# A cast to a DRAM scratch placed 5 steps later in the program, and its transposes 7 steps later

## The chip, the cores and the metric

The kernel runs on 1 core of one Trainium2 chip. The metric is the device time of one execution in microseconds (us). The core's engines are TensorE (PE, with PEld for its weight loads), VectorE (DVE), ScalarE (ACT), GpSimd (POOL) and SyncE (SP). Each works off its own queue in order.

## The reference

Two stages follow each other: a causal convolution along the sequence with 7 taps, whose weights are a softmax over the taps and one set for each of 8 heads (24 channels each), and a feed-forward block with a SiLU gate.

```python
def _attn_ref(x, weight):                 # x: (8, 4096, 192), weight: (8, 7)
    B, S, D = x.shape
    H, K = weight.shape
    group = D // H
    w = softmax(weight)                   # over the 7 taps
    x_pad = np.concatenate([np.zeros((B, K - 1, D)), x], axis=1)
    idx = np.arange(S)[:, None] + np.arange(K)[None, :]
    x_unf = x_pad[:, idx, :].reshape(B, S, K, H, group)
    return np.einsum('hk,bskhg->bshg', w, x_unf).reshape(B, S, D)

def _moe_ref(x, w_gate, w_val, w_out):    # x: (32768, 192), d_ff = 1536
    g = x @ w_gate
    silu = g * (1.0 / (1.0 + np.exp(-g)))
    return silu * (x @ w_val) @ w_out
```

## The kernel before, in words

The 32768 tokens are cut into 16 units of 2048 tokens (numbered from 0), each unit into 4 blocks of 512, and each block's feed-forward into 12 steps, one for each 128 of the 1536 hidden features. So there are 768 steps, 48 for a unit. Unit v begins at step 48v; a step's place in its block is called its step 0 to 11.

**A step** (`gate_val`, L768 to L789): six matmuls of 64x128 weights by 512 tokens, two at a time on the two row halves, fill the PSUM banks gate and val; ACT makes sig = silu(gate) (L786); DVE makes the product h = sig * val (L788). At steps 1, 4, 7 and 10 of a block a slot follows (`slot`, `down`, L803): 24 small matmuls that project products made earlier down to 192 channels. The slot at step 1 takes the products of the block before, among them that of its step 11; the one at step 4 ends that block, and ACT and DVE copy it (L860, L861) for the output DMA on SP (L864, three buffers). The banks gate and val have three buffers, so the matmuls of a step wait for the h of three steps before.

**The convolution** is made ahead of its use, and for unit 2 and the units from 4 on (`POOLED`) beside the steps, on ACT, DVE and POOL:

- `cast_x` (L590): POOL issues one DMA that reads the unit's x (2048 tokens and 16 ahead of them), turns it to 16 bit and writes it to a DRAM scratch xs (two buffers). For every second unit SP first writes zeros there (L583).
- `turn_x` (L605): SP issues transposes of 128 channels by 528 tokens from the scratch to SBUF, eight for a unit, in eight buffers for each of the two kinds (channels 0 to 127 of a block; channels 64 to 191, of which the upper half of a pair of blocks is used). `join_x` (L609) copies the second block's channels of a pair beside the first's, two for a unit.
- `queue_jobs` enters six jobs for a unit, in the order block 0, pair 0, block 1, block 2, pair 1, block 3. Each job sums seven shifted products. ACT makes the first into total (L682) and one or two more as part; DVE adds two by one instruction each, which reads the shifted x and total and writes total (L657, called a DVE step here); POOL adds ACT's parts (L632) and then makes the last two or three products itself (L647, piece) and adds each (L632). The last add writes the result in 16 bit, pxc for a block or y for a pair.
- `place` (L706): SP copies the results into the 64-row pieces that the gate and val matmuls read, 16 steps ahead of the block's first step.

**What sets the order.** Everything is recorded in one pass over the steps, and `seq` ties each instruction behind the one before it on its engine, so the place in the program is the order of each queue. `pooled_work` takes an ACT step and a DVE step from the lists at the steps 1, 7 and 10 of a block (ACT at step 4 too). POOL's part of a job is recorded when the DVE and ACT steps that it needs have been. `planned` (L722) puts a unit's cast, transposes and jobs on the plan by step number; in L957 the plan's entries of a step are recorded at that step's end. Before the change, for units from 4 on, the cast stands at step 48v - 115, the eight transposes and two joins at every second step from 48v - 105 to 48v - 87, and the jobs are entered at 48v - 89. The first ACT step of a unit's first job is recorded at 48v - 80 (48v - 83 for unit 4).

Of the kernel before, what the change touches and what calls it, by code (L numbers as in the profile page):

```python
# [10 lines left out]
def kernel(  # L11
# [564 lines left out]
    def cast_x(u):  # L576
        rows = XP + UT
        xs[u] = dpool.tile([rows, D], fp16, tag="xs", name="xs")
        flat = xs[u].rearrange("t d -> (t d)")
        skip = XP if u % upb == 0 else 0  # L580
        if skip:
            seq(
                nc.sync.dma_start(  # L583
                    out=flat[0 : XP * D].rearrange("(a n) -> a n", n=P),
                    in_=fill[0 : XP * D // P, :],
                )
            )
        n = (rows - skip) * D // P
        seq(
            nc.gpsimd.dma_start(  # L590
                out=flat[skip * D : rows * D].rearrange("(a n) -> a n", n=n),
                in_=bass.AP(
                    tensor=x_flat.tensor,
                    offset=(u * UT - XP + skip) * D,
                    ap=[[n, P], [1, n]],
                ),
            )
        )

    def turn_x(u, i, at):  # L600
        rows = xs[u][TB * i : TB * i + TB + XP]
        tiles = (x01, x12)[at // Q]
        tag = f"x{at // Q}"
        t = cpool.tile([P, TB + XP], fp16, tag=tag, name=tag, bufs=8)
        seq(nc.sync.dma_start_transpose(out=t, in_=rows[:, at : at + P]))  # L605
        tiles[u, i] = t

    def join_x(u, i):
        seq(nc.sync.dma_start(out=x12[u, 2 * i + 1][0:Q], in_=x12[u, 2 * i][Q:P]))  # L609
# [104 lines left out]
    def queue_jobs(u):  # L714
        for job in (
            ("block", 0), ("pair", 0), ("block", 1),
            ("block", 2), ("pair", 1), ("block", 3),
        ):
            conv_job(u, *job)
        placing.extend((u, i) for i in range(UB))  # L720

    def planned(v):  # L722
        s0 = ustep * v
        turns = (
            (0, 0), (0, Q), (1, Q), None, (1, 0), (2, 0), (2, Q), (3, Q), None, (3, 0)
        )
        if v == 2:
            cast, jobs = 21, 55
            times = (36, 36, 36, 38, 39, 39, 41, 41, 43, 43)
        elif v == 3:  # L730
            cast, jobs = 60, 56
            times = range(66, 86, 2)
        else:
            cast, jobs = s0 - 115, s0 - 89
            times = range(s0 - 105, s0 - 85, 2)
        plan.setdefault(cast, []).append(lambda: cast_x(v))
        for m, turn in enumerate(turns):
            if turn:
                todo = lambda turn=turn: turn_x(v, *turn)
            else:  # L740
                todo = lambda i=m // 8: join_x(v, i)
            plan.setdefault(times[m], []).append(todo)
        plan.setdefault(jobs, []).append(lambda: queue_jobs(v))
# [149 lines left out]
    for v in POOLED:  # L893
        planned(v)
# [106 lines left out]
```

## Time and profile before

| | us |
|---|---|
| median of 3 runs (lowest to highest) | 776.02 (775.38 to 777.03) |
| the profiled execution's own time | 777.99 |
| its span, first to last instruction | 776.2 |
| busy in the span: PE, DVE, ACT, POOL | 769.2, 706.2, 623.6, 597.6 |
| idle of POOL ahead of an add that waits for DVE (27 times) | 40.0 |
| wait of SP's queue at transposes, for casts (11 times) | 113.7 |
| a cast, from issue to landing, with zeros ahead or without (medians) | 6.7, 7.4 |

The granted TensorE clock was 0.999 of full speed. A row of the timeline gives the start in us from the span's start, the duration in us (of all where several equal ones are merged, "x2"), engine and line, output and input with their shapes, and in brackets the idle time ahead of it with what ended it. DVE rows overlap their neighbours by some 0.08 us, since the next instruction starts while the last one drains.

### The profile page before, as it was taken

The page shows a single profiled execution, that of the slowest core. Times are in us where ns is not written, and L with a number is a line of the kernel's source. Part 1 is how long each engine was busy: PE and PEld are TensorE (multiplying, and loading weights), DVE is VectorE, ACT ScalarE, POOL GpSimd, SP SyncE. Part 2 cuts the span into 40 slices and gives each one's busy share as a digit, 9 for nine tenths or more (in the row PEclk, how much of TensorE's full clock was granted, in tenths as well). Part 3 has the DMA queues.
Part 4 walks back from the last instruction along what each step waited for, and adds up shares of the span by engine and source line. Part 5 has one row for each costly group of instructions (what it writes and reads, how often), then busy time and mean ns, then how long its engine had stood idle before and what let it go on. Part 6 is the DMA issues. An engine that isn't in the chain of part 4 may idle for free.

```text
span 776.2 us, 27834 instructions
## 1 busy us (share of the span) xinstructions
PE 769.2 (99%) x11179; PEld 595.7 (77%) x11179; DVE 706.2 (91%) x1034; ACT 623.6 (80%) x1067; POOL 597.6 (77%) x551
## 2 busy tenths in 40 slices
PE   8999999999999999999999999999999999999997
PEld 5666666668878888788787888878888787887886
DVE  6677898999999999999999999999999999997775
ACT  6576888888888888888888888888888888876664
POOL 9100697799999999999999999999999999993000
PEclk9999999999999999999999999999999999999999
DMA  9959755745544535355343453635445344221211
GB/s 139 185 115 128 179 117 104 152 102 115 108 101 91 113 91 112 81 118 118 84 109 93 91 119 77 112 91 109 101 100 115 79 109 93 64 69 35 70 57 42
DMA packets 143652, 79.31 MB, mean 102 GB/s; under 512 B 89147, under 2 KB 143043, under 8 KB 143043
## 3 DMA queue, kind: packets, MB, share of 16 engines
q1 hardware_dynamic: 130690, 61.58, 35.3%
q0 software_dynamic: 12832, 15.96, 13.1%
q8 instruction: 87, 1.43, 0.8%
q14 instruction: 43, 0.34, 0.1%
HBM read 31.92 MB, written 37.83 MB: 90 GB/s over the span
## 4 chain that ended last, share of the span: by engine, by line
PE 98%; DVE 0%; issue 0%; ACT 0%; DVEq 0%
PE val L777 41%; PE acc L803 32%; PE gate L777 23%; PE warm L877 1%; PE turn L445 0%; DVE h L788 0%; PE cv L476 0%; PE cv L387 0%; PE acc L824 0%; ACT tme L405 0%; ACT wide L345 0%; ACT o_sb L969 0%; PE taps L332 0%; PE ctap L565 0%; PE tapbank L301 0%
## 5 line engine op out<-in xcount | busy, mean ns | idle before, releaser
L786 ACT ACTIVATE sig<-gate 128x512 f16<-128x512 f32 x768 | 458.6, 597 | 134.6 <-PE gate L777 82.0
L788 DVE TENSOR_TENSOR h<-sig,val 128x512 f16<-128x512 f16 x768 | 496.1, 682 | 60.3 <-PE gate L777 34.1
L777 PEld LDWEIGHTS <-w 64*128 64x128 f16 x4608 | 337.3, 110 | 137.0 <-issue 3.1
L777 PE MATMUL gate<-pxc,w 64*128 64x512 f16 x1872 | 438.8, 376 | 0.0
L777 PE MATMUL val<-pxc,w 64*128 64x512 f16 x1872 | 437.6, 376 | 0.1
L803 PE MATMUL acc<-wo,h 64*128 64x192 f16 x6096 | 330.4, 243 | 0.0
L803 PEld LDWEIGHTS <-h 64*128 64x128 f16 x6096 | 301.1, 94 | 30.3 <-issue 1.4
L632 POOL TENSOR_TENSOR total<-total,part 128x512 f32<-128x512 f32 x130 | 172.9, 1330 | 46.7 <-DVE total L657 40.0
L657 DVE SCALAR_TENSOR_TENSOR total<-x,both_taps,total 128x512 f32<-128x512 f16 x156 | 187.6, 1203 | 0.0
L632 POOL TENSOR_TENSOR total<-total,piece 128x512 f32<-128x512 f32 x104 | 147.6, 1419 | 8.7
L647 POOL TENSOR_SCALAR piece<-x,both_taps 128x512 f32<-128x512 f16 x182 | 150.8, 828 | 0.0
L777 PE MATMUL val<-xc,w 64*128 64x512 f16 x432 | 102.1, 376 | 0.5 <-issue 0.5
L777 PE MATMUL gate<-xc,w 64*128 64x512 f16 x432 | 102.1, 376 | 0.0
L682 ACT ACTIVATE part<-x,both_taps 128x512 f32<-128x512 f16 x130 | 92.8, 714 | 0.0
L632 POOL TENSOR_TENSOR pxc<-total,piece 128x512 f16<-128x512 f32 x52 | 67.8, 1303 | 4.3
L682 ACT ACTIVATE total<-x,both_taps 128x512 f32<-128x512 f16 x78 | 55.7, 714 | 0.0
L632 POOL TENSOR_TENSOR y<-total,piece 128x512 f16<-128x512 f32 x26 | 33.1, 1273 | 2.2
L861 DVE COPY o_sb<-acc 128x384 f32<-128x384 f32 x63 | 34.5, 547 | 0.0
L860 ACT COPY o_sb<-acc 128x384 f32<-128x384 f32 x63 | 29.7, 472 | 5.3 <-PE acc L803 5.3
L98 POOL DMA_DIRECT2D x<-in_x_dram x6 | 5.1, 873 | 24.5 <-ACT sig L786 24.5
L504 POOL COPY tm<-tm 128x1280 f16<-128x1280 f16 x2 | 2.5, 1251 | 19.2 <-DVE tm L493 19.2
L590 POOL DMA_DIRECT2D xs<-in_x_dram x13 | 7.2, 557 | 0.0
(67 smaller groups left out, 75.4 us busy)
## 6 DMA issues: line engine op xcount, KB each, us to landing
out_dram<-o_sb SPq DMA_DIRECT2D x63, 384.0 KB
pxc<-pxc SPq DMA_DIRECT2D x104, 64.0 KB
pxc<-y SPq DMA_DIRECT2D x104, 64.0 KB
xs<-in_x_dram POOLq DMA_DIRECT2D x7, 768.0 KB, 6.7
xs<-in_x_dram POOLq DMA_DIRECT2D x6, 774.0 KB, 7.4
x<-in_x_dram POOLq DMA_DIRECT2D x6, 480.0 KB, 9.1
scr<-tm SPq DMA_DIRECT2D x14, 130.0 KB
x<-x SPq DMA_DIRECT2D x26, 66.0 KB
```

Source lines behind the costliest of these rows:

```text
L590: nc.gpsimd.dma_start(out=flat[skip * D : rows * D].rearrange("(a n) -> a n", n=n), in_=bass.AP(tensor=x_flat.tensor, offset=(u * UT - XP ...
L632: nc.gpsimd.tensor_tensor(job["dst"] if k == K - 1 else total, total, part, op=ALU.add)
L647: nc.gpsimd.tensor_scalar(part, shifted(k), scalar1=job["tap"][:, k : k + 1], scalar2=1.0, op0=ALU.mult, op1=ALU.mult,)
L657: nc.vector.scalar_tensor_tensor(job["total"], shifted(k), job["tap"][:, k : k + 1], job["total"], op0=ALU.mult, op1=ALU.add,)
L682: nc.scalar.activation(part, shifted(k), AF.Copy, scale=job["tap"][:, k : k + 1])
L777: nc.tensor.matmul(o, w16[m][p0 : p0 + Q, k, e::E], xc[b][k][p0 : p0 + Q, 0:TB], start=(k == 0), stop=(k == SL - 1),)
L786: silu[n] = seq(nc.scalar.activation(sg, g, AF.Silu)).ins
L788: seq(nc.vector.tensor_tensor(hj, sg, v, op=ALU.mult))
L803: nc.tensor.matmul(acc[b][bank][:, s, :], hj[p0 : p0 + Q, ts(2 * bank + s, P)], wo16[p0 : p0 + Q, j, :], start=(not second and j == 0 and ...
L860: seq(nc.scalar.copy(o_sb[:, 0:2, :], acc[b][0]))
L861: seq(nc.vector.tensor_copy(o_sb[:, 2:4, :], acc[b][1]))
L877: nc.tensor.matmul(warm[:, 0:width], fill, fill.unsqueeze(1).to_broadcast([P, width // P, P]), start=True, stop=True, skip_group_check=True,)
```

## The change

For the units from 4 on the cast is recorded 5 steps later, at 48v - 110, and the transposes and joins 7 steps later, from 48v - 98 to 48v - 80. The step at which the jobs are entered stays.

```diff
@@ -731,8 +731,8 @@
             cast, jobs = 60, 56
             times = range(66, 86, 2)
         else:
-            cast, jobs = s0 - 115, s0 - 89
-            times = range(s0 - 105, s0 - 85, 2)
+            cast, jobs = s0 - 110, s0 - 89
+            times = range(s0 - 98, s0 - 78, 2)
         plan.setdefault(cast, []).append(lambda: cast_x(v))
         for m, turn in enumerate(turns):
             if turn:
```

On POOL each cast then stands behind the adds and products of one job more: for units from 5 on behind those of a pair job instead of ahead of them, and ahead of the next block job's. On SP the transposes and joins stand behind some outputs and placings that they stood ahead of. PE, DVE and ACT have the same instructions in the same order as before.

## The prediction

> **What bounds the kernel now.** I read the page first (shares and the chain that ended last), then the waits, then the timelines of VectorE (DVE), GpSimd (POOL) and ScalarE (ACT) side by side around single steps.
>
> ```profile
> PE 769.2 (99%) x11179; PEld 595.7 (77%) x11179; DVE 706.2 (91%) x1034; ACT 623.6 (80%) x1067; POOL 597.6 (77%) x551
> PE 98%; DVE 0%; issue 0%; ACT 0%; DVEq 0%
> PEld L803 <- DVE h L788: 0.4, 2, 0.2
> ```
>
> (The page's parts 1 and 4, and the waits of TensorE's weight loads.) TensorE holds 98% of the chain, so the change can only show as idle time of TensorE that comes or goes. The starts of the 768 sig rows (L786) on ACT say how much there is now. From step 140 on, equal steps of following 12-step blocks start 11.73 us apart, to 0.03 us, with eight exceptions: after step 145 (0.14 us late), after 157 (0.16), and after steps 376, 424, 472, 520, 568 and 616 (0.19 to 0.22 each, 1.25 in sum). At most these 1.55 us can be won, 0.2% of 776 us, and 0.2% is about what a measurement of this kernel can tell from no change.
>
> Both kinds of lost time come from one pairing: a conv step on DVE (L657, reads two SBUF tensors, 0.74 us alone) and a conv add or product on POOL. The first kind, from the timelines of POOL, DVE and ACT (start, duration, line, output and input, idle before):
>
> ```profile
> 155.67 1.27 POOL L632 TENSOR_TENSOR total<-total,part 128x512 f32<-128x512 f32 x1 [1.68 <-DVE total L657]
> 157.70 1.27 POOL L632 TENSOR_TENSOR total<-total,piece 128x512 f32<-128x512 f32 x1
> 157.71 1.80 DVE L657 SCALAR_TENSOR_TENSOR total<-x,both_taps,total 128x512 f32<-128x512 f16 x1
> 159.44 1.27 DVE L788 TENSOR_TENSOR h<-sig,val 128x512 f16<-128x512 f16 x2
> 161.19 0.60 ACT L786 ACTIVATE sig<-gate 128x512 f16<-128x512 f32 x1 [0.57 <-PE val L777]
> ```
>
> The add starts at 157.70 and ends at 158.97; the DVE step, issued 0.01 us from it, ends at 159.51, 0.54 after the add. It stands at a block's step 10, so the product h of step 11 ends at 160.11, and the down projection of the next block's step 1 needs it: TensorE stops for 0.14 us. The same follows at 169.58 (DVE step 1.82 us), giving the 0.16. The other kind:
>
> ```profile
> 430.78 0.56 POOL L590 DMA_DIRECT2D xs<-in_x_dram  x1
> 430.96 2.24 DVE L657 SCALAR_TENSOR_TENSOR total<-x,both_taps,total 128x512 f32<-128x512 f16 x1
> 431.35 2.98 POOL L632 TENSOR_TENSOR total<-total,part 128x512 f32<-128x512 f32 x2
> ```
>
> Here a DVE step arrives during the cast's issue, does not get in before the add behind it, and ends 0.55 us after that add (432.63): 2.24 us. The h behind it frees a PSUM bank for TensorE 0.2 us late. That is each of the six.
>
> Who wins when both arrive together? From the two timelines I listed all DVE steps by the distance from their start to that of a POOL add, with no cast between. The add won at every distance from -0.24 to +0.04 us; from +0.11 on the DVE step won and the add waited:
>
> ```profile
> 181.51 0.75 DVE L657 SCALAR_TENSOR_TENSOR total<-x,both_taps,total 128x512 f32<-128x512 f16 x1
> 181.62 1.77 POOL L632 TENSOR_TENSOR total<-total,piece 128x512 f32<-128x512 f32 x1
> ```
>
> **The change: instructions.** None is added or removed; the order on PE, DVE and ACT stays. On POOL each cast (0.56 us) passes one job's adds and products. On SP, eight transposes and two joins per unit move behind outs and places.
>
> **The change: data arrives later, and that is hidden.** Unit 10: its cast, issued at 383.65, moves behind the pair job's last add, to about 390.7. Landing takes 6.7 us (page, part 6), so the first transpose moves from 390.4 to 397.5. A join behind a transpose waits till about 3 us after that one's issue (169.6 to 172.5), so the tile is there at 400.5; ACT first reads it at 409.7: 9 us left. Unit 4: cast behind the add that ends at 106.88, transpose at 114, tile at 117, first read 124.0: 7 us. Unit 5: SP works off twelve transposes of unit 3 until 165.4 in either order; tile at about 169, first read 174.9: 6 us. If such cover were gone, each us late would stop ACT, and TensorE with it, for that us in every unit.
>
> SP now waits 113.7 us in all for casts. What queues behind that wait: the output of the block before, then the placing of the unit's third block. For unit 8 the transposes start at 397.5, the output goes at 401.6, the join at about 403.3, and the placing is issued by 407.5; block 34 starts at step 408, near 417.7. The output has three buffers, 36 steps. Both hidden; I count nothing.
>
> **The change: POOL's order, which is not hidden.** In unit 5's stretch, with the cast of unit 6:
>
> ```profile
> 195.25 0.55 POOL L590 DMA_DIRECT2D xs<-in_x_dram  x1
> 195.83 2.97 POOL L632 TENSOR_TENSOR total<-total,part 128x512 f32<-128x512 f32 x2
> ...
> 201.58 1.28 POOL L632 TENSOR_TENSOR y<-total,piece 128x512 f16<-128x512 f32 x1
> 203.55 1.27 POOL L632 TENSOR_TENSOR total<-total,part 128x512 f32<-128x512 f32 x1 [0.69 <-DVE total L657]
> 196.17 1.50 DVE L657 SCALAR_TENSOR_TENSOR total<-x,both_taps,total 128x512 f32<-128x512 f16 x1
> 202.04 1.37 DVE L657 SCALAR_TENSOR_TENSOR total<-x,both_taps,total 128x512 f32<-128x512 f16 x1
> ```
>
> The cast leaves the place ahead of 195.83 and goes into the idle 0.69 us ahead of 203.55, where POOL waits for DVE anyway. Unit 4's cast stands in just such a place now:
>
> ```profile
> 97.24 1.27 POOL L632 TENSOR_TENSOR y<-total,piece 128x512 f16<-128x512 f32 x1
> 97.54 1.52 DVE L657 SCALAR_TENSOR_TENSOR total<-x,both_taps,total 128x512 f32<-128x512 f16 x1
> 98.46 0.58 POOL L590 DMA_DIRECT2D xs<-in_x_dram  x1
> 99.21 1.27 POOL L632 TENSOR_TENSOR total<-total,part 128x512 f32<-128x512 f32 x1 [0.18 <-ACT sig L786]
> ```
>
> The DVE step ends at 99.06, 0.54 after the add, as without a cast; the cast costs POOL nothing. [...]
>
> So POOL gains 0.57 us per unit, and the six losses of the second kind end: -1.25 us. But POOL no longer lags; it is thrown back on DVE at each unit's second block job. Step by step: first add 195.26 to 196.54; DVE step of 196.17 ends 0.54 later, 197.08; second add held until 0.14 before that, ends 198.21 (1.59 less the earlier start); the rest takes 4.06 us as in the trace (198.80 to 202.86), ending 202.27; the DVE step of 202.04 ends at 202.82; the next job's first add starts 0.15 later, 202.96. Its second add follows 2.03 us later (155.67 to 157.70): 204.99. The DVE step of step 10 comes 2.93 us (three TensorE steps) after 202.04: 204.97. Distance +0.02 us, inside the stretch where the add won. The collision of 157.71 repeats, and its sequel (distance 0.00 at 169.58, now about +0.04) too. As POOL then stands to DVE as at 155.67, this recurs in each unit, for eleven units more (5 to 15), once a unit: the second half of a unit follows the row at 181.51, where DVE is 0.12 us late from its backlog and wins.
>
> A pair costs 0.30 us as measured at steps 145 and 157, up to 0.38 if the add starts 0.04 us later each time; the mean, 0.34, as the distance lies between. Sum: 11 x 0.34 = 3.7, less 1.25, +2.5 us (ends 2.05 and 2.9).
>
> The profiled execution took 777.99 us at a span of 776.2, 1.97 above the median of the runs; I add the difference to the median: 776.02 + 2.5 = 778.5, own range 777.9 to 779.2.
>
> **The rivals.** (1) The race goes to DVE: if the distance is over the unknown point between 0.04 and 0.11 us, there is no collision, and only the six losses go: 774.8. For it: my distances are good to some 0.03 us only. Against: the table's wins up to 0.04. (2) Both halves of a unit collide, if the row at 181.51 tips to POOL: 23 pairs of 0.36 less 1.25, +7: 783. Against: 0.11 us went to DVE once. (3) The shift makes no difference: POOL's lag finds another collision of the same size, 776. (4) Late tiles: the least cover, 6 us in unit 5, gone and 1 us over in three units: 779. Against: the wait rows above.
>
> **How the numbers follow.** Forecast 0.62; (1) 0.22, of which 0.12 is under 774.47 (0.2%) as the eighth, first pair may go too; (2) 0.07; (3) 0.06; (4) 0.03. Faster 0.12, same 0.10 + 0.06 = 0.16, slower 0.72. The range takes in the forecast and most of (1): 774.6 to 779.5.
>
> **What would show it.** Right: in the profile after, sig starts slip 0.14 to 0.2 us after steps 193 and 205, and every 48 steps from there; PEld L803 waits for DVE h about 24 times; no DVE step of 2.2 us is left; each cast from unit 6 on lies in the idle time ahead of a job's first add, 7 us later. Wrong: DVE steps of 0.75 us at those places, POOL idle 0.9 us ahead of two jobs a unit; or TensorE waits for ACT at unit starts.

## The result and the profile after

The changed kernel takes 779.13 us (median of 6 runs, 778.87 to 779.44) against 776.12 us (775.38 to 777.18) for the kernel before: a ratio of 1.0037, 95% interval 1.0027 to 1.0047. That is 3.0 us more; 2.5 was forecast. The profiled execution shown here took 778.87 us at a span of 777.1.

The page's parts 1 and 4 after:

```profile
PE 770.8 (99%) x11179; PEld 576.9 (74%) x11179; DVE 696.3 (90%) x1034; ACT 623.3 (80%) x1067; POOL 594.8 (77%) x551
PE 99%; ACT 0%; issue 0%; DVE 0%
```

DVE is busy for 9.9 us less and POOL for 2.8 us less, and the kernel is slower. Busy time of an engine off the path is no measure here, since a DVE step that waits for a POOL add counts as busy (1.85 us at 203.74 below, 0.74 alone). The starts of the sig rows show the loss. After step 140 they come late by 3.67 us in sum. It is one pair a unit: after steps 145 and 157 (0.14 each), 193 and 205 (0.19, 0.15), 241 and 253, and so on to 661, eleven pairs in all (one turn is skipped, see the account of the terms below). Where they come from, in unit 5's stretch (timeline of POOL: start, duration, line, output and input; the cast is that of unit 6):

```profile
194.03 2.95 POOL L632 TENSOR_TENSOR total<-total,part 128x512 f32<-128x512 f32 x2
...
199.77 1.27 POOL L632 TENSOR_TENSOR y<-total,piece 128x512 f16<-128x512 f32 x1
200.99 0.55 POOL L590 DMA_DIRECT2D xs<-in_x_dram  x1
201.74 1.26 POOL L632 TENSOR_TENSOR total<-total,part 128x512 f32<-128x512 f32 x1 [0.21 <-DVE total L657]
203.00 0.68 POOL L647 TENSOR_SCALAR piece<-x,both_taps 128x512 f32<-128x512 f16 x1
203.77 1.27 POOL L632 TENSOR_TENSOR total<-total,piece 128x512 f32<-128x512 f32 x1
```

The same stretch on DVE, and the sig row that follows on ACT:

```profile
200.81 0.79 DVE L657 SCALAR_TENSOR_TENSOR total<-x,both_taps,total 128x512 f32<-128x512 f16 x1
201.84 1.98 DVE L788 TENSOR_TENSOR h<-sig,val 128x512 f16<-128x512 f16 x3 [0.25 <-PE gate L777]
203.74 1.85 DVE L657 SCALAR_TENSOR_TENSOR total<-x,both_taps,total 128x512 f32<-128x512 f16 x1
205.51 0.68 DVE L788 TENSOR_TENSOR h<-sig,val 128x512 f16<-128x512 f16 x1
```

```profile
207.26 1.89 ACT L786 ACTIVATE sig<-gate 128x512 f16<-128x512 f32 x3 [0.62 <-PE val L777]
```

The cast lies in POOL's idle time: where 0.69 us stood ahead of this add, 0.21 us are left beside the cast. The add starts 0.14 us after the DVE step's end (201.60). The next add (203.77) starts 0.03 us after the DVE step of step 10 (203.74; the forecast was 0.02), and the DVE step ends at 205.59, 0.55 after the add. The h behind it is late, and the sig at 207.26 is 0.19 us behind its time.

How long a DVE step waits does not say alone what it costs; its place in the block does. The profile before has 32 DVE steps of over 1.7 us. Two stand at step 10 of a block and are followed by the first pair of late starts. The six of 2.2 us, at step 1 behind a cast, bring the six late starts of 0.2 us. The other 24 stand at step 1 or 7 and no late start follows, as behind this one at step 1 (step 241; DVE, then POOL, in the profile before):

```profile
254.82 1.86 DVE L657 SCALAR_TENSOR_TENSOR total<-x,both_taps,total 128x512 f32<-128x512 f16 x1
```

```profile
254.86 1.27 POOL L632 TENSOR_TENSOR total<-total,piece 128x512 f32<-128x512 f32 x1
```

The changed kernel has fewer such steps, 22, and all of them stand at step 10, each with a late start behind it.

### The profile page after: what moved, and what is told of

Its sections match the earlier page's. It is cut to its first block, busy times and chain, and to the rows that moved or that the text cites. A ratio compares the mean times of both kernels' runs of the same rounds, so it can differ in the third digit from the quotient of the medians.

```text
span 777.1 us, 27844 instructions
## 1 busy us (share of the span) xinstructions
PE 770.8 (99%) x11179; PEld 576.9 (74%) x11179; DVE 696.3 (90%) x1034; ACT 623.3 (80%) x1067; POOL 594.8 (77%) x551
## 4 chain that ended last, share of the span: by engine, by line
PE 99%; ACT 0%; issue 0%; DVE 0%
PE acc L803 33%; PE gate L777 33%; PE val L777 31%; PE warm L877 1%; PE turn L445 0%; PE cv L476 0%; PE cv L387 0%; PE acc L824 0%; ACT tme L405 0%; ACT wide L345 0%; ACT o_sb L969 0%; PE taps L332 0%; PE ctap L565 0%; PE tapbank L301 0%; DVE fill L92 0%
## 5 line engine op out<-in xcount | busy, mean ns | idle before, releaser
L777 PEld LDWEIGHTS <-w 64*128 64x128 f16 x4608 | 316.7, 110 | 148.1 <-issue 3.1
L803 PE MATMUL acc<-wo,h 64*128 64x192 f16 x6096 | 323.1, 243 | 0.0
L803 PEld LDWEIGHTS <-h 64*128 64x128 f16 x6096 | 289.7, 94 | 39.5 <-DVE h L788 2.3
L632 POOL TENSOR_TENSOR total<-total,part 128x512 f32<-128x512 f32 x130 | 169.1, 1301 | 51.1 <-DVE total L657 37.7
L657 DVE SCALAR_TENSOR_TENSOR total<-x,both_taps,total 128x512 f32<-128x512 f16 x156 | 170.0, 1090 | 0.0
L647 POOL TENSOR_SCALAR piece<-x,both_taps 128x512 f32<-128x512 f16 x182 | 153.9, 846 | 0.0
L632 POOL TENSOR_TENSOR total<-total,piece 128x512 f32<-128x512 f32 x104 | 142.5, 1370 | 8.7
L632 POOL TENSOR_TENSOR pxc<-total,piece 128x512 f16<-128x512 f32 x52 | 70.3, 1351 | 4.3
```

Source lines behind the costliest of these rows:

```text
L632: nc.gpsimd.tensor_tensor(job["dst"] if k == K - 1 else total, total, part, op=ALU.add)
L647: nc.gpsimd.tensor_scalar(part, shifted(k), scalar1=job["tap"][:, k : k + 1], scalar2=1.0, op0=ALU.mult, op1=ALU.mult,)
L657: nc.vector.scalar_tensor_tensor(job["total"], shifted(k), job["tap"][:, k : k + 1], job["total"], op0=ALU.mult, op1=ALU.add,)
L777: nc.tensor.matmul(o, w16[m][p0 : p0 + Q, k, e::E], xc[b][k][p0 : p0 + Q, 0:TB], start=(k == 0), stop=(k == SL - 1),)
L803: nc.tensor.matmul(acc[b][bank][:, s, :], hj[p0 : p0 + Q, ts(2 * bank + s, P)], wo16[p0 : p0 + Q, j, :], start=(not second and j == 0 and ...
```

## The experiments

Three accounts were set against each other: P, the time comes from where the cast stands among POOL's adds; S, it comes from SP's queue; L, it comes from x reaching SBUF later. What DVE and POOL shut each other out of is called the port pair in the expectations. Each time below stands beside the runs of the kernel before on the same chip. "Late" is the sum of late sig starts after step 140 in the profile.

| kernel | median us | before beside it | ratio, 95% interval | late, us |
|---|---|---|---|---|
| changed kernel | 779.13 | 776.12 | 1.0037 (1.0027 to 1.0047) | 3.67 |
| cast alone later | 792.05 | 776.72 | 1.0207 (1.0184 to 1.0230) | 14.2 |
| transposes alone later | 776.34 | 776.72 | 0.9994 (0.9985 to 1.0003) | 0.99 |
| cast at 48v - 122 | 777.75 | 776.72 | 1.0014 (1.0005 to 1.0023) | 0.33 |
| changed kernel and memsets | 775.24 | 776.72 | 0.9980 (0.9971 to 0.9989) | 0 |
| kernel before and memsets | 777.62 | 776.28 | 1.0015 (1.0007 to 1.0024) | 2.50 |
| cast at 48v - 122 from unit 6 on | 775.70 | 776.28 | 0.9994 (0.9986 to 1.0003) | 0.32 |
| both 5 steps later | 779.63 | 776.28 | 1.0034 (1.0022 to 1.0046) | 3.66 |

### The cast alone, and the transposes alone

```diff
-            cast, jobs = s0 - 115, s0 - 89
+            cast, jobs = s0 - 110, s0 - 89
```

> Only the cast moves (48v - 110); the transposes stay at 48v - 105. Theory P (the time comes from where the cast stands among POOL's adds): the whole effect, 2.0 to 3.2 us over the kernel before, and pairs of late sig starts (0.14 to 0.2 us) at step 1 of two following blocks once a unit. Rival S (SP's queue: transposes, outputs and placings in another order): within 0.6 us of before. Rival L (x reaches SBUF later): the first transpose still waits for the cast's landing, so it would show too, but as idle time of ACT at its first conv step of a unit, 1 us or more at a time, not as late products at DVE.

```diff
-            times = range(s0 - 105, s0 - 85, 2)
+            times = range(s0 - 98, s0 - 78, 2)
```

> Only the transposes and joins move (48v - 98); the cast stays at 48v - 115. P: within 0.6 us of before, with the six late starts of 0.2 us at step 40 of a unit as before. S: 2 to 3.2 us over before. L: nothing, since the tiles come only some 5 us later and ACT reads them 9 us after that.

The transposes alone make no difference that the interval tells from none, as P and L said, and S falls as the cause of the change's 3 us. (Of the six late starts of 0.2 us that were expected to stay, this profile has three, and two of 0.06; the second profile of the kernel before, below, bears on that.) The cast alone costs 15.3 us, which none of the three had. Its pairs of late starts are there (0.18 after step 193, 0.15 after 445), but most of the loss is something else. The waits of SP's queue and of TensorE in this run (total us, times, longest):

```profile
SPq L605 <- DMA xs<-in_x_dram: 178.9, 11, 19.6
```

```profile
PE val L777 <- DMA pxc<-y: 2.8, 4, 1.1
PE val L777 <- DMA pxc<-pxc: 2.5, 8, 0.7
PE gate L777 <- DMA pxc<-pxc: 1.6, 1, 1.6
PE gate L777 <- DMA pxc<-y: 0.8, 3, 0.3
```

SP waits for casts 178.9 us, against 113.7 before and 59.2 in the changed kernel. TensorE waits for placed blocks, which it does in neither of those. The late starts say which: 11.6 of the 14.2 us come at the steps 11, 12, 23 and 24 of a unit, where its second and third block begin (and another 3.1 us ahead of step 140, where unit 2's second block begins). With the transposes left at 48v - 105, the placing of a unit's second block is recorded behind the first three of them, and that of its third block behind all transposes and joins but the last; both wait with them for the later cast. For units 2 and 4 to 13 the last copy of these placings is issued 1.2 to 2.6 us ahead of the block's first sig; in the kernel before it is 5.4 us or more. SP's timeline for unit 8's second block, whose first step is 396:

```profile
405.26 1.14 SPq L605 DMA_TRANSPOSE x<-xs  x1
406.51 1.42 SPq L864 DMA_DIRECT2D out_dram<-o_sb  x1
407.98 2.65 SPq L605 DMA_TRANSPOSE x<-xs  x2
410.75 0.52 SPq L706 DMA_DIRECT2D pxc<-pxc  x1
411.31 1.23 SPq L706 DMA_DIRECT2D pxc<-y  x2
412.59 0.60 SPq L706 DMA_DIRECT2D pxc<-pxc  x1
```

The pieces land only as the block begins: the sigs after steps 395 and 396, at 414.4 and 415.6, are 0.15 and 0.52 us late.

### Both 5 steps later

```diff
-            cast, jobs = s0 - 115, s0 - 89
-            times = range(s0 - 105, s0 - 85, 2)
+            cast, jobs = s0 - 110, s0 - 89
+            times = range(s0 - 100, s0 - 80, 2)
```

> Cast and transposes both 5 steps later (48v - 110, 48v - 100), so the gap of 10 steps between them is that of before. The cast alone cost 15 us. Theory Q (the cast alone was that slow because the placing of a unit's second block stands behind the waiting transposes on SP; from 48v - 100 on it stands ahead of them): as the changed kernel, 2 to 3.5 us over before, no wait of TensorE for pxc. Rival (the shorter gap itself): as the changed kernel too or faster; if the lateness of the transposes' data had cost the 15 us, here it would cost as much again.

779.63 us: as the changed kernel, with 3.66 us late after step 140 against 3.67. No wait of TensorE for pxc is shown. Another 0.62 us of late starts stand ahead of step 140, after steps 119 and 120, where unit 2's third block begins; its last placing copy is issued 1.5 us ahead of that block's first sig. The gap between cast and transposes is the 10 steps of before, so the gap is not what matters; from 48v - 100 on the second block's placing stands ahead of the transposes, and that is what the transposes' part of the change does. It keeps the later cast from costing 15 us, and by itself it makes no difference that these runs show.

### A small memset on POOL, with the change and without

```diff
             while job["parts"]:
                 add(*job["parts"].pop(0))
+                if len(on_act) == 1:
+                    seq(nc.gpsimd.memset(nudge, 0.0))
```

> The changed kernel with one small POOL instruction more (memset of 128x128 f32 to a tile that nobody reads) behind the first add of each job that has one part from ACT, 26 in all, some 0.1 to 0.2 us each. P: the second add of these jobs then starts 0.1 to 0.2 us after the DVE step of step 10, which wins the port pair; the pairs of late starts go, and the kernel with more work is 2.0 to 3.7 us faster than the changed one (775.4 to 777) and at or under the kernel before. S and L: no change from the changed kernel, or slower by the added POOL time.

> The kernel before with the same 26 small memsets on POOL (0.20 us each as measured). P: here the cast still stands in POOL's way ahead of the pair job, and POOL loses 0.2 us more in each half of a unit, so the collision of the DVE step of step 1 with the add behind the cast comes earlier and in every unit: 0.5 to 1.2 us slower than the kernel before, the opposite of what the memsets did to the changed kernel. Rival N (the memsets help as such, for instance because POOL's adds come later everywhere): 1 to 2 us faster than the kernel before here too.

This is the test of the race itself. With 26 more instructions the changed kernel takes 775.24 us, 1.5 us less than the kernel before beside it, where without them it took 3.0 us more. (The two were measured on different chips; the times themselves, 775.24 and 779.13, are 3.9 us apart.) POOL's timeline with them, at unit 5's second block job:

```profile
202.22 0.55 POOL L590 DMA_DIRECT2D xs<-in_x_dram  x1
202.98 1.26 POOL L633 TENSOR_TENSOR total<-total,part 128x512 f32<-128x512 f32 x1 [0.21 <-DVE total L660]
204.19 0.20 POOL L644 MEMSET nudge<- 128x128 f32 x1
204.37 0.69 POOL L650 TENSOR_SCALAR piece<-x,both_taps 128x512 f32<-128x512 f16 x1
205.14 1.71 POOL L633 TENSOR_TENSOR total<-total,piece 128x512 f32<-128x512 f32 x1
```

And DVE's:

```profile
204.98 0.75 DVE L660 SCALAR_TENSOR_TENSOR total<-x,both_taps,total 128x512 f32<-128x512 f16 x1
```

The second add comes 0.16 us after the DVE step instead of 0.03. The DVE step takes 0.75 us, the add waits (1.71), and from step 140 to the end no sig start is late by more than 0.02 us, the first pair included.

Without the change the same memsets cost 1.3 us (777.62 against 776.28), a little over the 0.5 to 1.2 expected. In that profile each of the units 5 to 12 has a late start of 0.20 to 0.23 us at its step 40, and a second of 0.08 us nine steps on. DVE and POOL there, behind unit 8's cast:

```profile
289.73 2.23 DVE L660 SCALAR_TENSOR_TENSOR total<-x,both_taps,total 128x512 f32<-128x512 f16 x1
```

```profile
289.55 0.55 POOL L590 DMA_DIRECT2D xs<-in_x_dram  x1
290.12 2.97 POOL L633 TENSOR_TENSOR total<-total,part 128x512 f32<-128x512 f32 x2
```

So the memset helps where it moves an add past a DVE step, and costs time in the kernel whose cast stands in POOL's way. That rules out N, and S and L too: the order of SP's queue is the same in the changed kernel with the memsets and without, and its waits for casts are 65.4 us against 59.2.

### The cast earlier

```diff
-            cast, jobs = s0 - 115, s0 - 89
+            cast, jobs = s0 - 122, s0 - 89
```

> The cast 7 steps earlier than before (48v - 122), the transposes as before. On POOL it then stands between the last add of a unit's last block job and the first add of the next unit's first. P, by replaying POOL's and DVE's rows with the measured durations: the cast meets no DVE step there, and POOL has time to make up for it, so all late starts after the first pair go: 1.25 us faster than before, 774.9. S: as before (the transposes find the scratch ready, and what waits behind them goes earlier, hidden anyway). L: as before. If any place other than the old one is bad: 2 to 3 us slower.

The late starts after step 140 went as P said: only the first pair is left (0.33 us). But the kernel is 1.0 us slower. Two new late starts, 0.80 and 0.52 us, stand after steps 131 and 132, where unit 2's last block begins. TensorE's timeline there, and SP's ahead of it:

```profile
147.16 0.37 PE L777 MATMUL gate<-pxc,w 64*128 64x512 f16 x1 [0.24 <-DMA pxc<-y]
147.86 0.37 PE L777 MATMUL val<-pxc,w 64*128 64x512 f16 x1 [0.33 <-DMA pxc<-pxc]
```

```profile
133.94 9.42 SPq L512 DMA_DIRECT2D scr<-tm  x8
143.40 0.39 SPq L520 DMA_DIRECT2D scr<-tm  x1
143.89 0.52 SPq L706 DMA_DIRECT2D pxc<-pxc  x1
```

Unit 5's cast, issued at 132.97, now runs beside the eight scratch writes of unit 3. Their issue takes 9.42 us (4.98 in the kernel before), and the placing behind them comes at 143.89 instead of 140.1. In the next run units 4 and 5 kept their old place:

```diff
-            cast, jobs = s0 - 115, s0 - 89
+            cast, jobs = s0 - (122 if v > 5 else 115), s0 - 89
```

> The kernel before with the cast at 48v - 122 for the units from 6 on only; units 4 and 5 keep 48v - 115. P: the 1.4 us that the earlier cast cost once, at unit 2's last block, came from unit 5's cast running beside unit 3's scratch writes, so they go, and the six late starts of 0.2 us stay away: 0.7 to 1.3 us faster than the kernel before. Rival: an earlier cast costs something in every unit that the late starts don't show: as before or 1 us slower.

The two late starts are gone, the eight scratch writes take 4.97 us to issue again, and 0.32 us of late starts remain. The time is 775.70 against 776.28, which the interval (0.9986 to 1.0003) does not tell from no change, less than the 0.7 to 1.3 us expected. The next run offers a reason.

### The kernel before once more

> The kernel before, unchanged, for a second profile. If the profile shown of it was one with a late start and many late sig starts, this one has its first steps up to 1 us earlier or less than 1.55 us of late starts after step 140, and the measured 3.0 us between the kernels agrees with the steps; if not, 1 us of the difference lies outside the steps.

This run took 775.64 us at a span of 773.9. It has none of the six late starts at step 40: late in sum 0.61 us after step 140 (the first pair and one more after steps 673 and 685), against 1.59 in the profile shown first. Unit 11's cast and the DVE step beside it, the place that took 2.24 us there (DVE, then POOL):

```profile
429.38 1.49 DVE L657 SCALAR_TENSOR_TENSOR total<-x,both_taps,total 128x512 f32<-128x512 f16 x1
```

```profile
428.45 0.55 POOL L590 DMA_DIRECT2D xs<-in_x_dram  x1
429.03 2.98 POOL L632 TENSOR_TENSOR total<-total,part 128x512 f32<-128x512 f32 x2
```

Here POOL stands some 0.7 us earlier against DVE: the DVE step comes 0.35 us after the add's start, not 0.39 before it, and waits 0.7 us less. The first sigs come earlier as well: step 24 at 36.74 us, 38.04 in the first profile. So the kernel before is not one rhythm but at least two, and the one that the prediction read loses 1 us more than the other. How often each occurs is not known from two profiles.

## Why the prediction was right

**The race.** Working, places and sign held: cast hidden in POOL's idle time, POOL thrown back on DVE at the second block job, distance 0.03 us (0.02 forecast), POOL's add winning, a pair of late starts after steps 193 and 205 and then each unit. The first rival, the race lost, is what the memset made of the kernel, so it was a real alternative. How near it was shows in the profiles of all ten runs: with no cast between, no add won that started more than 0.04 us behind the DVE step, and the DVE step won from 0.05 us on, here in the run with the cast alone (DVE, then POOL):

```profile
377.51 0.74 DVE L657 SCALAR_TENSOR_TENSOR total<-x,both_taps,total 128x512 f32<-128x512 f16 x1
```

```profile
377.56 1.83 POOL L632 TENSOR_TENSOR total<-total,piece 128x512 f32<-128x512 f32 x1
```

The measured distance lies within 0.02 us of that point, and the prediction held its distances good to some 0.03 us only. That the race went the forecast way was therefore likely by the working, but also luck.

**The terms.** Eleven pairs beyond the first at 0.34 us were forecast, 3.7 us. There are ten, and they measure 3.24 us in sum, 0.32 each: after step 397 the pair moves by 24 steps to the unit's other half and skips one turn, as the add behind the DVE step of 440.09 came 0.09 us after it and lost. The prediction had the other half of a unit free of collisions throughout. The term that was mis-sized is the gain of 1.25 us. It was read from one profile, and the second profile of the kernel before has none of it. With 0.61 to 1.59 us late before and 3.67 after, the steps make 2.1 to 3.1 us, and 3.0 were measured. The two terms erred in opposite directions, the pairs 0.5 us too dear and the gain too large by up to its whole size, so that the sum of 2.5 came so near is in part luck.

**What was counted at nothing.** The transposes' arrival was hidden as worked out: unit 10's first transpose stands at 396.87 (397.5 forecast), its first read on ACT at 410.01. The placing of unit 8's third block is issued by 407.3 (407.5 forecast). SP's waits for casts fell from 113.7 to 59.2 us. What was not weighed is why this was harmless: the prediction named only the third block's placing behind the wait, and did not say that the transposes' move puts the second block's placing ahead of it. With the cast alone later, where that placing stands behind the wait and the third block's behind more of it, the kernel took 15.3 us more than before.

**The skill on the port pair.** The Trainium skill (SBUF — State Buffer, "SBUF: two separate sides") says that DVE and GpSimd share a pair of SBUF ports by a lock that is exclusive and held for the whole instruction. The rows agree: the DVE step of 203.74 ends 0.55 us after the add that won. The same section says that a DMA from GpSimd's queue is locked out from writing its descriptors while DVE runs an instruction in a 2-port mode. That case was not looked for in these runs. The two-input DVE steps here do not hold the cast up: the cast at 200.99 is issued beside the DVE step of 200.81 and takes its 0.55 us, and the next add starts 0.14 us after the DVE step.

**Not as written:** TensorE's weight loads at L803 are shown waiting for DVE's h 12 times (2.3 us), not some 24; the other late starts carry another label or none.

## What to carry to other kernels

Where two engines share a lock and one of them runs at the pace of the kernel, moving one instruction of 0.55 us can set up a collision that repeats in every round; look up how far apart the two instructions start, and where the distance is no further from the tipping point (here 0.04 to 0.05 us) than the working is good for, treat it as a coin. Ask also where in the round the collision falls: here the same wait cost 0.14 to 0.19 us at one step of a block and nothing at two others. Losses read from one profile of such a kernel may be those of one of its rhythms: take a second profile before a gain is booked on them. When a load is moved, list what its queue holds up as well as what it feeds: here the harmless half of the change was the one that kept the other from costing 15 us.

## What the runs showed of the hardware

- A DVE step that reads two SBUF tensors (0.74 us alone) and a POOL add shut each other out for the whole instruction. In the ten profiles the add won up to a start 0.04 us after the DVE step's (254.82 in the profile before), and the DVE step won from 0.05 us on (377.51 in the run with the cast alone). A losing DVE step ends 0.54 to 0.56 us after the add; a losing add ends 1.13 us after the DVE step, as if it (1.27 us alone) had begun 0.14 us before that step's end.
- A DVE step that arrives while POOL issues the cast, with an add ready to start 0.02 us behind the cast, does not get in before that add, even 0.4 us ahead of its start (2.24 us at 430.96 in the profile before). Where the add behind the cast still waits for that DVE step, the step runs beside the cast in its 0.74 us (the DVE step at 484.56, 0.08 us after the cast's start, in the changed kernel).
- More work can be faster: with 26 memsets of 0.20 us on POOL the changed kernel took 775.24 us instead of 779.13, and the 156 DVE steps took 147 us in sum instead of 170.
- The first 24 steps vary by 1.6 us between profiles (step 24 at 36.74 to 38.39 us) for equal instructions; what makes them vary was not looked into.
